# Retention by quarters of the array from the fifth chunk on, and one block's two layers interleaved

## The chip, the cores and the metric

One core of a Trainium2 chip. The metric is the device time of one execution in microseconds (us); the kernel before was run three times. Engines: TensorE (PE) multiplies, its weight loads beside it (PEld), VectorE (DVE), ScalarE (ACT), GpSimd (POOL), SyncE (SP), which here only issues DMA transfers.

## The reference

```python
def _attn_ref(q, k, v):                    # 8 batches, 8 heads, 576 tokens, 64 wide
    scores = scale * np.matmul(q, k.transpose(0, 1, 3, 2))
    gamma = 1.0 - 2.0 ** (-5.0 - np.arange(H))
    Dmat = np.where(rel >= 0, gamma ** rel, 0.0)        # rel = position i - position j
    return np.matmul(scores * Dmat, v)

def _moe_ref(x, w_in, w_out):              # x: 4608 tokens x 512; w_in 512 x 2048; w_out 2048 x 512
    h = x @ w_in
    return (h * np.cos(h)) @ w_out

def reference(**kwargs):
    attn_out = _attn_ref(...)              # retention, per batch and head
    x = attn_out.transpose(0, 2, 1, 3).reshape(4608, 512)
    return _moe_ref(x, moe_w_in, moe_w_out)
```

Retention with decay is computed in chunks of tokens: a token sees its own chunk through masked scores, and everything before through a state (a 64 x 64 matrix per head) that is carried from chunk to chunk and begins anew with each batch. The decay is folded into q (`UQ`) and v (`WV`).

## The kernel before

**Work and tiling.** The 4608 tokens are 36 chunks of 128 (`g` = 0 to 35) and 9 blocks of 512 (`j` = 0 to 8). A batch has 576 tokens, so a batch ends within a chunk or a block. Retention writes its output, transposed, in bf16 into the ring `XT` (1536 tokens). A block's first layer is `mlp1(j, dt)` for 16 strips `dt` of `w_in`: four matmuls into one PSUM bank, then ACT's `Sin(h + pi/2)` into `CB`, then DVE's product with h into `GT`. The second layer is `plain2` in blocks 0 and 1 (16 groups of four matmuls, four open outputs, each of which holds a bank), and `mlp2` from block 2 on, seven half-size products instead of eight with sums prepared by DVE (`ssum`, and `tsum` for the weights). First-layer groups take turns through the banks of `MM` (four) that no output holds; `take` and `free` move them.

**Two forms of retention.** Batches 0 and 1 (`b`, chunks `r` = 0 to 4, the last of 64 tokens) run with whole-chunk matmuls: `scores`, `rest` (outputs), `state_mm` and `state_copy`. Their k and q arrive as "quads" (`quad`: four neighbouring tokens per partition, so a packet holds 1 KB), are cast (`quad_cast`), turned by PE (`quad_turn`), and k is turned back by PE (`back`), since the state needs it both ways. The chunk of 64 tokens is turned by `turn`, or by DMA.

From chunk `G0` = 9 on a chunk is loaded by `load_g` (one row of 256 B per token and head), cast by POOL (`casts_g`: k, q, v), turned by a DMA on SP's queue (`turn_dma`), and computed by `quarters(g, n)`, called through `visit`: the array works as four 64 x 64 parts; in one call the outputs of chunk `g` and the scores and state of chunk `n` = g + 1 are woven together. Afterwards DVE masks two halves of the scores and adds two states, ACT copies two halves of the outputs to `XT` (`xt`) and casts two states to bf16 (`SM`, `SN`); these steps wait in `todo` and are put out by `flush`. The next visit reads the scores and the states.

**What sets the order.** Each engine runs its instructions in the order in which `emit` writes them; semaphores tie the engines. SP's queue holds loads and turns in one order. `pump` puts out pending loads as far as loading buffers (16) are free and no more than `AHEAD` = 9 of them (12 later) hold data not yet cast; three make a chunk. `prep(g)` is casts, turn and pump. In block 0's second layer the order is a table by group number `n` (casts, turns, scores of batch 1); in block 1's first layer strips are split at token 192 or 320 around batch 1's `rest`; in block 1's second layer a visit follows groups 1, 5, 9 and 13. In block `j` >= 2 two visits stand in the first layer, after strips 4 and 10, and two in `mlp2`, ahead of product 6 and ahead of product 4.

```python
            if fn == self.load_g and sum(self.busy) + n > (AHEAD if a[0] < 4 * 4 + 2 else AHEAD + 3):
                return
...
        for dt in range(16):
            self.mlp1(j, dt)
            self.flush(2)
            self.steps1(j, dt)
            if dt % 3 == 0 and dt < 12:
                self.prep(g + 3 + dt // 3)
            if dt in (4, 10) and g < NG:
                self.visit(g + dt // 6)
```

Of the kernel before, what the change touches and what calls it, by code (L numbers as in the profile page):

```python
# [13 lines left out]
DM = H_ * D_  # L14
# [10 lines left out]
AHEAD = 9  # L25
SLOT = (0, 1, 2, 3, 8, 4, 5, 6, 7)
G0 = 9
# [6 lines left out]
def slot(b, r):  # L34
    return SLOT[(NCH * b + r) % NR]

# [4 lines left out]
def gslot(g):  # L41
    return SLOT[(g - G0 + 2 * NCH) % NR]

# [4 lines left out]


def ck_of(r):  # L50
    return min(CH, S_ - CH * r)
# [92 lines left out]
class _Kernel:  # L144
# [154 lines left out]
    def load(self, b, r, xs="kqv"):  # L299
        ck = ck_of(r)  # L300
        for x in xs:
            src = bass.AP(self.src[x], (b * H_ * S_ + CH * r) * D_, [[D_, ck], [S_ * D_, H_], [1, D_]])
            self.fetch((x, b, r), src, [[D_, H_], [1, D_]], ck)
# [18 lines left out]
    def quad(self, x, b, c):  # L322

        src = bass.AP(self.src[x], (b * H_ + 2 * c) * S_ * D_, [[4 * D_, 128], [S_ * D_, 2], [1, 4 * D_]])
        self.fetch((x, b, "c", c), src, [[4 * D_, 2], [1, 4 * D_]], 128)
# [21 lines left out]
    def kcast(self, eng, b, r):  # L347
        ck, i = ck_of(r), slot(b, r)
        t, bt = self.use(("k", b, r))
        o, a = bass.AP(self.KQ[i], 0, [[2 * DM, ck], [1, DM]]), bass.AP(t, 0, [[DM, ck], [1, DM]])  # L350
        self.copy(eng, o, a, [bt], [self.bKB[i]])

    def casts_g(self, g):
        i, r = gslot(g), column(g)
        t, bt = self.use(("k", g))
        h4 = [[DM, CH], [4 * D_, 2], [D_, 4], [1, D_]]
        self.copy("pool", self.heads(self.KQ[i], 0, 2 * DM, CH), bass.AP(t, 0, h4), [bt], [self.bKB[i]])
# [3 lines left out]
        self.s.op("pool", lambda e: e.tensor_tensor(o, a, w, ALU.mult), reads=[bt, self.bUQ], writes=[self.bQB[i]])  # L361
# [3 lines left out]
        self.s.op("pool", lambda e: e.tensor_tensor(o2, a2, w2, ALU.mult), reads=[bt, self.bWV], writes=[self.bVB[i]])  # L365
# [5 lines left out]
    def decay(self, eng, x, b, r):  # L371
        ck, i = ck_of(r), slot(b, r)
        t, bt = self.use((x, b, r))
        d, off, pitch, bd, w, bw = ((self.KQ[i], DM, 2 * DM, self.bQB[i], self.UQ, self.bUQ) if x == "q"
                                    else (self.VB[i], 0, DM, self.bVB[i], self.WV, self.bWV))
        o, a, g = (bass.AP(d, off, [[pitch, ck], [D_, H_], [1, D_]]), bass.AP(t, 0, [[DM, ck], [D_, H_], [1, D_]]),
                   bass.AP(w, r * H_, [[2 * NCH * H_, ck], [1, H_], [0, D_]]))
        self.s.op(eng, lambda e: e.tensor_tensor(o, a, g, ALU.mult), reads=[bt, bw], writes=[bd])  # L378
# [4 lines left out]
    def casts(self, b, r, engs=("pool", "pool", "pool")):  # L383
        self.kcast(engs[0], b, r)
        self.decay(engs[1], "q", b, r)
        self.decay(engs[2], "v", b, r)

    def turn_dma(self, i, ck=CH):
        s = self.s
        s.dma("sp", f"t{i}", lambda e: e.dma_start_transpose(  # L390
            self.kqt(i, 0, ck, 2 * NP), bass.AP(self.KQ[i], 0, [[2 * DM, ck], [1, 2 * DM]])),
            reads=[self.bKB[i], self.bQB[i]], writes=[self.bKT[i], self.bQT[i]])

    def turn(self, b, r, x, eng, bank=None):
        ck, i = ck_of(r), slot(b, r)
        off, c0, bs, bd = (0, 0, self.bKB[i], self.bKT[i]) if x == "k" else (DM, NP, self.bQB[i], self.bQT[i])
        m, bm = bank or self.bank()
        self.group([(bass.AP(m, c * CH, [[512, 128], [1, ck]]),
                     bass.AP(self.KQ[i], off + c * 128, [[2 * DM, ck], [1, 128]]),
                     bass.AP(self.ID, 0, [[128, ck], [1, ck]]),  # L400
                     dict(start=c == 0, stop=c == NP - 1)) for c in range(NP)],
                   [bs, self.bID], [bm])
        self.copy(eng, self.kqt(i, c0, ck, NP), bass.AP(m, 0, [[512, 128], [CH, NP], [1, ck]]), [bm], [bd])

    def quad_cast(self, eng, x, b, c):

        t, bt = self.use((x, b, "c", c))
# [12 lines left out]
    def quad_turn(self, x, b, c, i, eng, bank=None):  # L420
# [6 lines left out]
        s0 = slot(b, 0)  # L427
        off = s0 * W + (c if x == "k" else NP + c) * CH
        t = self.copy(eng, bass.AP(self.KQT, off, [[NR * W, 128], [W, 4], [4, 32], [1, 4]]),
                      bass.AP(m, 0, [[512, 128], [32, 4], [1, 32], [CH, 4]]), [bm], [Buf()])  # L430
        for u in (self.bKT if x == "k" else self.bQT)[s0:s0 + 4]:
            u.w.append(t)

    def back(self, b, r, eng, bank=None):

        i = slot(b, r)
# [33 lines left out]
    def scores(self, b, r, own=True):  # L470
        s, ck, i = self.s, ck_of(r), slot(b, r)
        sc, bsc = zip(*(zip(self.SC, self.bSC) if own else [self.bank(), self.bank()]))
        mms = []
        for c in range(NP):
            for hp in range(2):
                base = 64 * hp * NR * W + i * W + c * CH
                mms.append((
                    bass.AP(sc[hp], c * CH, [[512, ck], [1, ck]]),
                    bass.AP(self.KQT, base, [[NR * W, 64], [1, ck]]),
                    bass.AP(self.KQT, base + NP * CH, [[NR * W, 64], [1, ck]]),  # L480
                    dict(start=c == 0, stop=c == NP - 1)))
        self.group(mms, [self.bKT[i], self.bQT[i]], list(bsc))
        for hp in range(2):
            p3 = [[512, ck], [CH, NP], [1, ck]]
            s.op("dve", lambda e: e.tensor_tensor(
                bass.AP(self.RT[r % 2][hp], 0, p3), bass.AP(sc[hp], 0, p3),
                bass.AP(self.MK, 0, [[CH, ck], [0, NP], [1, ck]]), ALU.mult),
                reads=[bsc[hp], self.bMK], writes=[self.bRT[r % 2][hp]])

    def rest(self, b, r, bank=None, eng="act", state=True):  # L490
# [19 lines left out]
        if r:  # L510
            reads += [self.bSB[(r - 1) % 2], self.bQT[i]]
# [590 lines left out]
```

## Time and profile before

| | us |
|---|---|
| median of three runs | 296.84 (296.74 to 297.48) |
| the profiled execution | 296.34 |
| its span, first to last instruction | 294.6 |
| PE busy | 283.1 |
| DVE busy | 215.0 |
| ACT busy | 173.2 |
| POOL busy | 94.2 |

The profiled execution ran 0.5 us under the median, and 1.74 us of it lie outside the span. Matmuls are pipelined and their ends modelled, so PE's busy time is no measure of its work; the distance between the starts of groups is. In the timelines a row gives start, length, engine, line, operation, output and inputs, shape and count; brackets give the idle time before it and what ended it. In the rows of DMA queues stand packets, MB and the share of the 16 DMA engines' time: q0 carries the weights, q1 SP's loads and turns, q10 the output. In rows of windows the last three columns are the granted clock, DMA share and GB/s.

### The profile page before, as it was taken

To read this page: it belongs to the slowest core of one execution; us is meant where nothing else is said; L and a number is where in the kernel's file an instruction comes from. 1 tells how busy PE (TensorE), PEld (TensorE's weight loads), DVE (VectorE), ACT (ScalarE), POOL (GpSimd) and SP (SyncE) were. 2 spreads that over 40 slices of the span, in tenths; PEclk is the share of its full clock that TensorE was granted. 3 is DMA by queue.
4 is the path that set the end of the run, shared out by engine and by line. 5 is a ranking of instruction groups with operands and counts; after the bars stand their busy time and mean duration, and the time that the engine had idled before them with its cause. 6 is when DMAs were issued, how large, how long until landed. Compare 5 with 4: busy or idle time off the path is not lost.

```text
span 294.6 us, 8326 instructions
## 1 busy us (share of the span) xinstructions
PE 283.1 (96%) x3523; PEld 180.3 (61%) x3554; DVE 215.0 (73%) x466; ACT 173.2 (59%) x344; POOL 94.2 (32%) x119
## 2 busy tenths in 40 slices
PE   6899999899999999999999999999999999999996
PEld 3474455555554478547854785478547854784485
DVE  3667657767766797579758975897589658956973
ACT  6798424887446854585458445844585358536720
POOL 3570227664516520760076007600760030000000
PEclk9999999999999999999999999999999999999999
DMA  6999999999999999999999957997690170013013
GB/s 210 258 181 198 217 312 198 311 187 185 229 201 235 204 198 229 257 202 188 200 242 230 180 136 169 199 189 164 181 181 0 38 145 2 3 36 109 0 38 107
DMA packets 142325, 49.70 MB, mean 169 GB/s; under 512 B 125904, under 2 KB 141264, under 8 KB 142288
## 3 DMA queue, kind: packets, MB, share of 16 engines
q1 hardware_dynamic: 129280, 35.53, 64.4%
q10 hardware_dynamic: 8784, 9.44, 10.1%
q0 software_dynamic: 4224, 4.19, 8.7%
q8 instruction: 28, 0.46, 0.7%
q14 instruction: 9, 0.07, 0.1%
HBM read 36.70 MB, written 9.44 MB: 157 GB/s over the span
## 4 chain that ended last, share of the span: by engine, by line
PE 78%; DMA 13%; SPq 2%; ACT 2%; issue 1%; POOL 1%; DVE 1%; DVEq 0%
PE mm L461 52%; PE mm L463 17%; DMA ld<-in_v_dram 7%; DMA ld<-in_q_dram 4%; PE st L709 3%; PE sc L709 2%; SPq L290 2%; DMA win<-in_moe_w_in_dram 2%; PE po L709 2%; POOL vb L378 1%; PE sc L461 1%; ACT sb L342 1%; PE sc L463 0%; ACT xt L342 0%; ACT kq L342 0%
## 5 line engine op out<-in xcount | busy, mean ns | idle before, releaser
L554 DVE TENSOR_TENSOR gt<-mm,cb 128x512 bf16<-128x512 f32 (+3 forms) x156 | 99.1, 646 | 33.2 <-ACT cb L552 32.4
L552 ACT ACTIVATE cb<-mm,c_pih 128x512 bf16<-128x512 f32 (+3 forms) x156 | 100.6, 654 | 36.4 <-PE mm L463 35.7
L461 PE MATMUL mm<-xt,win 128*128 128x512 bf16 (+3 forms) x445 | 113.3, 362 | 2.8 <-issue 1.9
L461 PEld LDWEIGHTS mm<-xt,win 128*128 128x128 bf16 x468 | 43.4, 98 | 45.2 <-ACT xt L342 0.6
L463 PE MATMUL mm<-xt,win 128*128 128x512 bf16 (+3 forms) x156 | 56.6, 363 | 0.1
L342 POOL CAST kq<-ld 128x512 bf16<-128x512 f32 (+1 forms) x29 | 17.7, 609 | 113.8 <-PE mm L463 96.5
L461 PE MATMUL mm<-wout,gt 128*128 128x256 bf16 (+1 forms) x257 | 49.3, 310 | 1.0 <-issue 1.0
L461 PE MATMUL mm<-ts,ss 128*128 128x256 bf16 x240 | 35.4, 273 | 0.0
L461 PEld LDWEIGHTS mm<-wout,gt 128*128 128x128 bf16 x264 | 24.8, 98 | 12.0 <-DVE gt L554 0.4
L342 ACT ACTIVATE u<-mm 128x512 f32<-128x512 f32 x21 | 12.5, 597 | 32.2 <-PE mm L463 32.2
L361 POOL TENSOR_TENSOR kq<-ld,uq 128x512 bf16<-128x512 f32 x27 | 28.1, 1042 | 6.0 <-DMA ld<-in_q_dram 6.0
L365 POOL TENSOR_TENSOR vb<-ld,wv 128x512 bf16<-128x512 f32 x27 | 28.3, 1049 | 4.1 <-DMA ld<-in_v_dram 4.1
L643 DVE TENSOR_TENSOR osb<-mm,u 128x512 f32<-128x512 f32 x20 | 13.8, 688 | 18.8 <-PE mm L463 11.2
L463 PE MATMUL mm<-wout,gt 128*128 128x256 bf16 (+1 forms) x88 | 27.4, 311 | 0.0
L342 ACT ACTIVATE xt<-po 128x256 bf16<-128x256 f32 (+1 forms) x34 | 14.0, 413 | 21.9 <-PE st L709 15.7
L463 PEld LDWEIGHTS mm<-xt,win 128*128 128x128 bf16 x156 | 15.2, 98 | 16.0
L461 PEld LDWEIGHTS mm<-ts,ss 128*128 128x128 bf16 x240 | 23.0, 98 | 2.8
L750 DVE TENSOR_TENSOR rt<-sc,mh 128x256 bf16<-128x256 f32 x54 | 21.2, 416 | 4.4 <-PE st L709 3.2
L463 PE MATMUL mm<-ts,ss 128*128 128x256 bf16 x80 | 21.8, 273 | 0.0
L576 DVE TENSOR_TENSOR ss<-gt 128x512 bf16<-128x512 bf16 x56 | 20.7, 417 | 0.0
L760 DVE TENSOR_TENSOR pf<-sc,pf 128x256 f32<-128x256 f32 x42 | 17.6, 419 | 1.1
L709 PE MATMUL po<-rt,vb 64*64 64x64 bf16 x216 | 13.4, 202 | 0.1
(155 smaller groups left out, 384.1 us busy)
## 6 DMA issues: line engine op xcount, KB each, us to landing
out_dram<-osb ACTq DMA_DIRECT2D x35, 256.0 KB, 3.3
ld<-in_k_dram SPq DMA_DIRECT2D x32, 256.0 KB, 4.4
ld<-in_q_dram SPq DMA_DIRECT2D x32, 256.0 KB, 5.0
ld<-in_v_dram SPq DMA_DIRECT2D x32, 256.0 KB, 5.9
win<-in_moe_w_in_dram POOLq DMA_DIRECT2D x4, 512.0 KB, 6.1
wout<-in_moe_w_out_dram POOLq DMA_DIRECT2D x4, 512.0 KB, 15.0
ld<-in_k_dram SPq DMA_DIRECT2D x8, 128.0 KB, 4.1
ld<-in_q_dram SPq DMA_DIRECT2D x8, 128.0 KB, 3.9
```

Of the source, the lines that this page charges most:

```text
L342: fn = (lambda e: e.activation(o, x, AF.Copy)) if eng == "act" else (lambda e: e.tensor_copy(o, x))
L361: self.s.op("pool", lambda e: e.tensor_tensor(o, a, w, ALU.mult), reads=[bt, self.bUQ], writes=[self.bQB[i]])
L365: self.s.op("pool", lambda e: e.tensor_tensor(o2, a2, w2, ALU.mult), reads=[bt, self.bWV], writes=[self.bVB[i]])
L461: self.nc.tensor.matmul(o, a, b, **kw)
L463: return s.done("pe", self.nc.tensor.matmul(o, a, b, **kw), reads, writes)
L552: s.op("act", lambda e: e.activation(ci, mi, AF.Sin, bias=self.C_PIH.ap(), scale=1.0), reads=[bm, self.bC], writes=[self.bCB[i]])
L554: s.op("dve", lambda e: e.tensor_tensor(bass.AP(self.GT, dt * TB + o0, [[16 * TB, 128], [1, n]]), mi, ci, ALU.mult), reads=[bm, self.bCB[i ...
L576: self.s.op("dve", lambda e: e.tensor_tensor(self.s_(k, d), a, b, op), reads=rd, writes=[S[k - 1][p]])
L643: self.s.op("dve", lambda e: e.tensor_tensor(o, m, x, ALU.add), reads=[bm, self.bU[u]], writes=[self.bOSB[i]])
L709: inst = self.nc.tensor.matmul(o, a, c, **kw)
L750: s.op("dve", lambda e: e.tensor_tensor(bass.AP(self.RT[n % 2][x], 0, p3), bass.AP(self.SC[x], 0, p3), bass.AP(self.MH, 0, [[64, 128], [0, ...
L760: s.op("dve", lambda e: e.tensor_tensor(self.PF[t].ap(), u, self.PF[1 - t].ap(), ALU.add), reads=[self.bSU[t], self.bPF[1 - t]], writes=[s ...
```

## The change

Batch 0 keeps its first four chunks in the whole-chunk form; its state then passes to the quarters' form (`state_over`, four small ACT copies). From chunk 4 on (`G0` = 4) every chunk is loaded by `load_g` and computed by `quarters`. Chunks 4 and 5 are turned by PE, all later ones by DMA. The quads, turns back, scores and outputs of batch 1 in the whole-chunk form are gone. Blocks 0 and 1 now hold ten visits instead of four: chunk 4's scores, 4 with 5, and 5's outputs in block 0's second layer; then seven in block 1 (V5 to V11, the first only the scores and state of chunk 6).

Block 1's layers are interleaved by an order written out: `F` is the first layer for the first 256 tokens of a strip, `S` for the second 256, `P` a quarter of an output's sum in the second layer, `V` a visit with the `prep` of the chunk three further, `T` a weight sum, `O` the store of an output kept back. Outputs of block 0 go to `U` and `OSB` and are stored later, the last of them during block 2's first layer. Prefetch is 12 buffers, 6 and 12 again, by chunk. In block 2 the visits stand at strips 9 and 15, ahead of product 4 and behind it; in block 3 at strips 7 and 12 and as before. At the start, POOL's decay of chunk 2's v stands behind the second to fourth loads of `w_in` instead of between them.

```diff
-AHEAD = 9
-SLOT = (0, 1, 2, 3, 8, 4, 5, 6, 7)
-G0 = 9
+def ahead(g):
+    return 12 if g < 8 else 6 if g < 21 else 12
+G0 = 4
...
+ORDER1 = """
+F0 F1 F2 F3 F4 F5 F6 P00 F7 F8 F9 F10 V5 P01 F11 F12 F13 F14 F15 P02 T0 P10 T1 P11 V6 P12 T2 P03 T3 P13
+V7 S0 S1 S2 S3 S4 S5 S6 P20 V8 S7 S8 S9 S10 P21 O3 S11 S12 V9 S13 S14 S15 P22 T4 P30 T5 P31 V10
+P32 O0 T6 P23 T7 O0 V11 P33
+"""
...
+    def state_over(self, eng):
+        sn, bsn = self.SN[(G0 - 1) % 2], self.bSN[(G0 - 1) % 2]
+        ws = []
+        for b in range(2):
+            for hp in range(2):
+                ws.append(self.copy(eng, bass.AP(sn, 64 * b * NP * D_ + hp * D_, [[NP * D_, 64], [2 * D_, 2], [1, D_]]),
+                                    bass.AP(self.ST, 64 * hp * 512 + 2 * b * D_, [[512, 64], [D_, 2], [1, D_]]),
+                                    [self.bST], [Buf()]))
+        bsn.w = ws
...
     def mlp2(self, j, visits):
+        def visit(k):
+            if k in visits:
+                self.visit(visits[k])
+                self.flush(6)
...
-        for g in visits[:1]:
-            self.visit(g)
-        self.flush(6)
+        visit(2)
         self.product(bs, 6, False, False)
...
-        for g in visits[1:]:
-            self.visit(g)
-        self.flush(6)
+        visit(7)
         if not last:
             self.product(bs, 4, False, True)
             i21 = self.osb()
...
+        visit(4)
         self.store(i22, j, 1, 1)
...
         for n in range(16):
-            self.plain2(0, n % 4, n // 4, None)
+            self.plain2(0, n % 4, n // 4)
+            if 2 <= n < 10:
+                self.tsum("dve", *T.pop(0))
+            if n == 7:
+                self.turn(4, "k", "act", XY[0])
+                self.turn(4, "q", "dve", XY[1])
+                self.casts_g(5)
+            if n == 11:
+                self.quarters(None, 4)
+                self.flush()
+            if n == 13:
+                self.turn(5, "k", "act", XY[0])
+                self.turn(5, "q", "dve", XY[1])
+                o += [self.out2(0, st, eng) for st, eng in ((0, "act"), (1, "dve"))]
+                for g in (6, 7):
+                    self.casts_g(g)
+                    self.turn_dma(g)
                 self.pump()
+            if n == 14:
+                self.quarters(4, 5)
+                self.flush()
             if n == 15:
+                self.quarters(5, None)
+                self.flush()
+                o += [self.out2(0, st, eng) for st, eng in ((2, "dve"), (3, "act"))]
...
+        for u in ORDER1.split():
+            n = int(u[1:])
+            if u[0] == "V":
+                self.quarters(n if n > 5 else None, n + 1)
+                self.prep(n + 3)
+            elif u[0] == "P":
+                self.plain2(1, n // 10, n % 10)
+                if n % 10 == 3:
+                    o.append(self.out2(1, n // 10, "act"))
+            elif u[0] == "O":
+                self.put2(*o.pop(n))
+            elif u[0] == "T":
+                self.tsum("dve", *T[n])
+            else:
+                m1([n], (0 if u[0] == "F" else 256, 256), 1)
+            self.flush(4)
+        self.flush()
         for j in range(2, NTB):
             g = 4 * j + 4 if j < NTB - 1 else NG
+            at = {2: (9, 15), 3: (7, 12)}.get(j, (4, 10))
             for dt in range(16):
                 self.mlp1(j, dt)
                 self.flush(2)
                 self.steps1(j, dt)
+                if o and dt % 3 == 1:
+                    self.put2(*o.pop(0))
...
-                if dt in (4, 10) and g < NG:
-                    self.visit(g + dt // 6)
-            self.mlp2(j, range(g + 2, min(g + 4, NG)))
+                if dt in at and g < NG:
+                    self.visit(g + at.index(dt))
+            self.mlp2(j, {} if g == NG else dict(zip((7, 4) if j == 2 else (2, 7), (g + 2, g + 3))))
```

More of the change, by code (lines that the diff above doesn't have):

```diff
@@ L468, in idle, with scores @@
                      dict(start=True, stop=True)) for _ in range(n)], [self.bIDLE], [bm])
-    def scores(self, b, r, own=True):
-        s, ck, i = self.s, ck_of(r), slot(b, r)
+    def scores(self, r, own=True):
+        s = self.s
         sc, bsc = zip(*(zip(self.SC, self.bSC) if own else [self.bank(), self.bank()]))
@@ L510, in rest @@
         if r:
[L511 removed]
+            reads += [self.bSB[(r - 1) % 2], self.bQT[r]]
         self.group(mms, reads, [bpo])
[L513 to L522 removed]
@@ L890, in pump @@
             else:
-                n = 3 if fn == self.load_g or fn == self.load and len(a) == 2 else 1
+                n = 3 if fn == self.load_g else 1
                 if any(self.busy[(self.n_ld + i) % NL] for i in range(n)):
                     return
-                if fn == self.load_g and sum(self.busy) + n > (AHEAD if a[0] < 4 * 4 + 2 else AHEAD + 3):
+                if fn == self.load_g and sum(self.busy) + n > ahead(a[0]):
                     return
```

313 lines of the change are left out of this document (103 added, 210 removed).

## The prediction

> **What bounds the kernel now.** I read the page first, then the stage boundaries in the timeline of TensorE (PE), then one stage piece by piece, then the DMA queues by window. The page:
>
> ```profile
> span 294.6 us, 8326 instructions
> PE 283.1 (96%) x3523; PEld 180.3 (61%) x3554; DVE 215.0 (73%) x466; ACT 173.2 (59%) x344; POOL 94.2 (32%) x119
> PEclk9999999999999999999999999999999999999999
> ```
>
> PE is the bound, at full clock. "Busy 96%" does not say that it works at its peak, so I price the change by the starts of matmul groups. Boundaries, from the timeline of PE and, for the last two, the chain of waits:
>
> ```profile
> 33.12 0.81 PE L461 MATMUL mm<-wout,gt 128*128 128x512 bf16 x3
> 33.98 0.81 PE L461 MATMUL mm<-wout,gt 128*128 128x512 bf16 x3
> 54.51 0.41 PE L461 MATMUL mm<-xt,win 128*128 128x192 bf16 x3
> 72.27 0.81 PE L461 MATMUL mm<-wout,gt 128*128 128x512 bf16 x3
> 89.26 0.81 PE L461 MATMUL mm<-xt,win 128*128 128x512 bf16 x3
> 148.21 0.59 PE mm L461 x2
> 177.62 0.59 PE mm L461 x2
> ```
>
> Block 0's second layer starts at 33.12, block 1's first layer at 54.51, its second at 72.27, block 2 at 89.26. One group of four 512-column matmuls takes 0.864 us (33.12 to 33.98). From block 2 on, a block takes 29.41 us (148.21 to 177.62), with four visits; the change leaves that rhythm alone except in block 2. So the time is decided by when block 2 starts, plus what block 2 loses. Before 33.12 the changed program keeps PE's order; POOL's third decay and the weight loads swap places in one queue, and four ACT copies replace two, each beside first-layer groups with free ACT time. I cost that at nothing; if a weight load came late it would be tenths.
>
> The pieces, from the timelines of PE, ACT and DVE:
>
> ```profile
> 20.66 0.49 PE L461 MATMUL mm<-xt,win 128*128 128x256 bf16 x3
> 21.09 0.49 PE L461 MATMUL mm<-xt,win 128*128 128x256 bf16 x3
> 21.31 1.77 ACT L552 ACTIVATE cb<-mm,c_pih 128x256 bf16<-128x256 f32 x4
> 21.82 1.72 DVE L554 TENSOR_TENSOR gt<-mm,cb 128x256 bf16<-128x256 f32 x4 [0.43 <-ACT cb L552]
> 42.14 0.33 PE L461 MATMUL po<-ident,qs 128*128 128x128 bf16 x3
> 42.59 0.81 PE L461 MATMUL mm<-wout,gt 128*128 128x512 bf16 x3
> 82.16 0.38 PE L463 MATMUL mm<-wout,gt 128*128 128x512 bf16 x1
> 82.47 0.22 PE L709 MATMUL st<-rt,vb 64*64 64x64 bf16 x2
> 83.13 0.76 DVE L750 TENSOR_TENSOR rt<-sc,mh 128x256 bf16<-128x256 f32 x2 [0.95 <-PE st L709]
> 83.44 0.59 PE L461 MATMUL mm<-wout,gt 128*128 128x512 bf16 x2 [0.16 <-issue]
> 83.44 0.38 ACT L342 ACTIVATE xt<-po 128x256 bf16<-128x256 f32 x1 [1.93 <-PE st L709]
> 83.72 0.38 ACT L342 ACTIVATE xt<-st 128x256 bf16<-128x256 f32 x1
> 83.81 0.94 DVE L760 TENSOR_TENSOR pf<-sc,pf 128x256 f32<-128x256 f32 x2
> 84.25 0.42 ACT L342 ACTIVATE sm<-pf 128x256 bf16<-128x256 f32 x1 [0.16 <-DVE pf L760]
> L342 ACT ACTIVATE osb<-mm 128x512 f32<-128x512 f32 x12 | 7.1, 595 | 7.2 <-PE mm L463 7.2
> ```
>
> Read from them: a 256-column first-layer group takes 0.437 us of PE. Its bank is free 1.61 us after its start: Sin begins 0.645 later (20.66 to 21.31), the product 0.51 after that, and lasts some 0.43. Two turns by PE (eight 128-column matmuls) take 0.45 (42.14 to 42.59). A whole visit takes 0.85: the group at 82.16 ends its slot at 82.38, and the next group, whose first record is missing, started one matmul before 83.44, at 83.22. From a visit's start (82.47) its tokens stand in XT after 1.64 (83.72 + 0.38) and the state SM after 2.2 (84.25 + 0.42).
>
> **The change, part by part.** *Block 0's second layer.* Before, 33.12 to 54.51 is 21.4 us, of which the 16 groups are 13.8. The rest is batch 1's turns back and forth, four chunks' scores and waits. After: 13.8; turns of chunks 4 and 5 by PE, 2 x 0.45; scores and state of chunk 4 alone, about 0.45 (half a visit); one whole visit 0.85; the outputs of chunk 5 alone, about 0.5. That is 16.5. Two waits are new: the last visit needs the state of the visit one group (0.864) earlier, which takes 2.2, so it stands some 0.5; and block 1's first group needs the tokens of that visit, 0.9 after PE could go on (1.64 against 0.75 of visit). Block 1 starts at 33.12 + 16.5 + 1.4 = 51.0, so **3.5 us earlier**.
>
> *Block 1.* Before, 54.51 to 89.26 is 34.75. After: 32 halves x 0.437 = 14.0; 16 groups x 0.864 = 13.8; the first visit (scores only) 0.5 and six whole ones x 0.85 = 5.1; together 33.4. The stalls follow from the order written out. Four banks at 1.61 sustain one half in 0.40, under PE's 0.437; but each open output holds one, and three banks sustain only one in 0.54. So F10, the fourth half behind P00, stands 0.3. After a visit DVE adds for 0.94 and ACT then casts two states (0.42 each) ahead of the queued Sins, while PE runs ahead: F14 and F15 stand 0.9 together, S5 and S6 0.6 (the visit before them adds and casts one state, not two), S10 0.4, S12 0.4. S0 follows its visit directly and stands 0.9 for the tokens. In all 3.5; block 1 takes 36.9, **2.15 us more**. Block 2 would start at 51.0 + 36.9 = 87.9, against 89.26.
>
> *Block 2.* Its last visit is moved behind product 4. The casts of the visit before are queued on ACT behind the copy of that product's result (0.6, queued until the product ends), and the last visit's past part needs SM: 0.6 + 0.4 after the product's end, where PE gets there after 0.5. **0.6 us**. The delayed stores cost ACT only issue time, beside its slack; the visits at dt 9 and 15 cost what they cost elsewhere.
>
> *DMA.* The last chunk that block 1 needs turned is 12, for the visit V11. Rows of the DMA queues by window (24 to 36, 57 to 79, 80 to 92), POOL's arrivals, and two windows of all engines:
>
> ```profile
> q0 software_dynamic: 1802, 1.78, 87.7%
> q1 hardware_dynamic: 1803, 0.66, 32.8%
> 28.93 0.60 POOL L342 CAST kq<-ld 64x512 bf16<-64x512 f32 x1 [7.53 <-DMA ld<-in_k_dram]
> 31.96 1.03 POOL L378 TENSOR_TENSOR kq<-ld,uq 64x512 bf16<-64x512 f32 x1 [2.42 <-DMA ld<-in_q_dram]
> 35.23 1.06 POOL L378 TENSOR_TENSOR vb<-ld,wv 64x512 bf16<-64x512 f32 x1 [2.23 <-DMA ld<-in_v_dram]
> q1 hardware_dynamic: 17213, 4.31, 93.9%
> q1 hardware_dynamic: 7097, 1.78, 109.5%
> q10 hardware_dynamic: 400, 0.72, 17.2%
> 36.00:44.00 8.00, 7.84 (x72) 4.25 (x72) 3.92 (x8) 1.76 (x5) 2.13 (x4) 1.00 1.15 306
> 60.00:72.00 12.00, 11.59 (x85) 6.49 (x82) 8.35 (x19) 9.78 (x21) 7.00 (x8) 1.00 0.96 196
> ```
>
> While the weights load (q0), the input queue (q1) gets one packet for each of theirs, 150 a microsecond: 512 packets every 3.0 to 3.3 us (28.93, 31.96, 35.23). Chunk 4 is now whole, 1024 packets for each of k, q, v (128 tokens x 8 heads of 256 B): k at 32.0, q at 38.3, cast by 39.4, and its turn by PE stands at 33.12 + 8 x 0.864 = 40.0. In time. v follows between 39.6 (at 782 a microsecond) and 45 (at 150); the 306 GB/s of 36 to 44 says that the weights end in it, and I take 41. Chunks 5 to 7 take 3 x 3072 packets at 782 a microsecond (17213 in 22 us), until 52.8; chunk 5's q lands near 43.6 and is wanted at 46. From there to chunk 12 turned lie six loads (8 to 13, since each turn is issued behind the next load) and seven turns, 18432 + 7168 = 25600 packets: 32.7 us, until 85.5; one output store (0.72 MB took 17.2% of 12 us, so 0.75 for 256 KB) and the landing add 1.1: 86.6. V11 stands at 51.0 + 35.3 = 86.3. So DMA and PE meet: I take 0.3 us of wait. Both ends: nothing, if 800 or more packets pass in a microsecond; at the 591 of 80 to 92 (7097 in 12 us, stores among them) 25600 packets take 43 us, 10 us late. I take the value near 782, since that window is as full of loads and turns and has almost no stores, as block 1 will.
>
> Against the change speaks the size of the packets: batch 1's k and q came as 1 KB packets and now come as 256 B; the window with 1 KB packets moved 306 GB/s beside the weights, the one without 196. The counts above hold that already. The Trainium skill, page "DMA: Bandwidth & Descriptors", section Specifications, puts the smallest transfer at line rate at 512 B, with a read-modify-write below it; the trace agrees in direction, 0.64 of the rate. By that rule alone (half of 306, an estimate) the five chunks' 2.6 MB of k and q would take 17 us where 196 GB/s gives 13.4, so V11 would wait some 4 us and the sum be 3.5 us worse, which is the late turns below at their far end.
>
> Sum: -3.5 + 2.15 + 0.6 + 0.3 = -0.45 us. The profiled execution took 296.34 us, 1.74 beyond its span and 0.5 under the median of the three runs, 296.84. I forecast against the median: **296.4 us**, no change that can be told; a measurement of this kernel can tell about 0.3%, 0.9 us.
>
> **The rivals.** *Turned chunks late (slower).* A turn waits for POOL's casts, sits in one queue with the loads, and now only two chunks are ahead where three were. For it: the sum meets at the edge already, and 80 to 92 was slower. Against it: SP's own issues fit. It decides below 780 packets a microsecond. At 745, 34.4 us bring chunk 12 at 88.3, 2.0 late: 298.1. At 715, the mean of both windows (24310 in 34 us), 3.4 late: 299.5.
>
> *The stalls in block 1 are smaller (faster).* The 2.6 us of bank waits come from queue orders that I followed step by step; if ACT's casts slip between the Sins, they go. Then V11 stands at 83.7, and DMA decides: at 830 packets a microsecond chunk 12 comes at 52.8 + 30.8 + 1.1 = 84.7 and 1.0 of wait comes back, with none of the 0.3: 296.4 - 2.6 - 0.3 + 1.0 = 294.5. Against it: the in-order queues leave little choice.
>
> *The head start doesn't come.* Chunk 4 or 5 late by 1 to 2 us, and block 1 starts at 52.5: 297.9.
>
> **How the numbers follow.** The forecast with its edges (295.6 to 297.3) 0.42; late turns 0.27; smaller stalls 0.26; no head start 0.05. Faster by over 0.3%: 0.25 of the third case and 0.07 of the forecast's lower edge, 0.32. Slower: nearly all late turns and half of the last, 0.28. Within: 0.40. Range 294.4 to 299.5: from just under the faster rival's time to the late turns at 715.
>
> **What would show it.** Right: block 1's first group at 51.0 +- 0.5, block 2's at 87.6 to 88.6, gaps of some 0.9 before F0 and S0, waits of ACT's and DVE's making at F10, F14, S5, and a gap of some 0.6 in block 2's last visit. Wrong by late turns: PE waiting in V7 to V11 for the turn's DMA. Wrong by the stalls: block 2 before 86.5. Wrong at the start: a first-layer group of block 0 not at its old time, or block 1 after 52.

## The result, and the profile after

The changed kernel takes 298.3 us (median of 11 executions, 297.25 to 299.72) against 296.73 us before (11 executions, 296.18 to 299.65): a ratio of 1.0051 [1.0026, 1.0076], slower by half a per cent. Timed once more on another occasion it was 298.73 against 296.44, 1.0068 [1.0040, 1.0096]. The forecast was 296.4, no change that can be told. The profiled execution took 297.25 us, 0.91 more than the profiled one before; it is the fastest of its 11, so 1.05 us of the median is not in it.

The head of the page after, and its input queue:

```profile
span 295.5 us, 8651 instructions
PE 284.7 (96%) x3694; PEld 180.6 (61%) x3694; DVE 215.9 (73%) x473; ACT 171.9 (58%) x351; POOL 97.4 (33%) x120
PEclk9999999999999999999999999999999999999999
q1 hardware_dynamic: 138048, 36.19, 68.9%
```

Nothing here tells where 0.9 us went: PE is the bound as before, at full clock. The boundaries and stalls do, from the timeline of PE (start, duration, work; in brackets what it waited for last):

```profile
50.89 0.50 PE L445 MATMUL mm<-xt,win 128*128 128x256 bf16 x3 [0.76 <-ACT xt L343]
...
56.45 0.28 PE L445 MATMUL mm<-xt,win 128*128 128x256 bf16 x1 [0.15 <-DVE gt L541]
...
60.84 0.28 PE L445 MATMUL mm<-xt,win 128*128 128x256 bf16 x1 [0.36 <-DVE gt L541]
...
69.04 0.39 PE L445 MATMUL mm<-xt,win 128*128 128x256 bf16 x2 [0.84 <-ACT xt L343]
...
72.28 0.28 PE L445 MATMUL mm<-xt,win 128*128 128x256 bf16 x1 [0.33 <-DVE gt L541]
...
87.87 0.39 PE L445 MATMUL mm<-xt,win 128*128 128x512 bf16 x1
...
112.04 0.50 PE L445 MATMUL mm<-ts,ss 128*128 128x256 bf16 x3 [0.57 <-DVE ss L563]
...
118.82 0.38 PE L445 MATMUL mm<-xt,win 128*128 128x512 bf16 x1
...
132.11 0.22 PE L692 MATMUL po<-kqt,sn 64*64 64x64 bf16 x2 [0.24 <-ACT sm L343]
...
148.87 0.38 PE L445 MATMUL mm<-xt,win 128*128 128x512 bf16 x1
```

Block 1 starts at 50.89 (54.51 before), and block 2 at 87.87 (89.26 before), 1.4 us earlier. Then block 2 takes 30.95 us and block 3 30.05, where they took 29.62 and 29.33 (and the later blocks 29.41 to 29.50); at 148.87 the kernel is 0.66 behind the one before (148.21), and from there every block takes what it took. So the gain was made where it was forecast, and given back, with interest, in the next two blocks. The row at 112.04 is a wait that the prediction doesn't have: 0.74 us by the distance between starts, where the bracket has 0.57, because it counts from the modelled end of the matmul before (waits without a row below are by starts, too). What was going on beside it, in the timeline of all engines:

```profile
109.21 3.11 DVE L563 TENSOR_TENSOR ss<-gt 128x512 bf16<-128x512 bf16 x4
...
109.42 1.10 POOL L356 TENSOR_TENSOR kq<-ld,uq 128x512 bf16<-128x512 f32 x1 [0.43 <-DMA ld<-in_q_dram]
...
110.48 1.22 POOL L360 TENSOR_TENSOR vb<-ld,wv 128x512 bf16<-128x512 f32 x1
```

Four of DVE's sums for product 7 take 3.11 us, where four without POOL beside them take 1.42 (a row of it below), while POOL multiplies q and v of chunk 17, which have just come from the DMA. The groups of DVE's sums from 100 to 146 us, first after, then before (busy time, mean ns of one):

```profile
L563 DVE TENSOR_TENSOR ss<-gt 128x512 bf16<-128x512 bf16 x16 | 8.1, 559 | 0.0
```

```profile
L576 DVE TENSOR_TENSOR ss<-gt 128x512 bf16<-128x512 bf16 x16 | 5.8, 418 | 0.0
```

And the windows of the second layers of blocks 2 and 3 (the column with 6.95 and 3.47 is POOL's busy time), first after, then before:

```profile
104.00:118.80 14.80, 13.88 (x236) 11.52 (x235) 13.24 (x31) 5.47 (x14) 6.95 (x7) 1.00 1.21 212
...
133.00:148.80 15.80, 15.80 (x242) 12.84 (x241) 12.78 (x33) 7.56 (x17) 3.47 (x4) 1.00 1.17 217
```

```profile
104.70:118.90 14.20, 14.15 (x242) 12.32 (x242) 11.48 (x31) 5.66 (x14) 0.86 (x1) 1.00 1.23 214
...
134.00:148.20 14.20, 14.16 (x234) 12.24 (x234) 11.60 (x31) 5.79 (x14) 0.00 (x0) 1.00 1.25 211
```

Before, the DMA was far enough ahead that POOL had nearly all its casts done in a block's first layer, where DVE forms only two of a block's sixteen sums, behind strip 14. The changed kernel's loads run later against its blocks, and POOL casts when the data come: in the second layer, beside the sums. None of the 112 sums in the profile before has a POOL operation beside it; in the profile after nine have.

The theories from here: **A**, the loss is work that the new order and the later loads put beside each other in blocks 2 and 3 (ACT's casts ahead of close visits, POOL's casts beside sums); **B**, in executions slower than the profiled one, turned chunks come late and PE waits for them in block 1.

### The profile page after: what moved, and what is told of

Read it like the earlier page. It is cut to its first block, busy times and chain, and to the rows that moved or that the text cites. A ratio compares the mean times of both kernels' runs of the same rounds, so it can differ in the third digit from the quotient of the medians.

```text
span 295.5 us, 8651 instructions
## 1 busy us (share of the span) xinstructions
PE 284.7 (96%) x3694; PEld 180.6 (61%) x3694; DVE 215.9 (73%) x473; ACT 171.9 (58%) x351; POOL 97.4 (33%) x120
## 4 chain that ended last, share of the span: by engine, by line
PE 86%; DVE 7%; ACT 3%; issue 1%; DMA 1%; POOL 0%; DVEq 0%; ACTq 0%; POOLq 0%
PE mm L445 58%; PE mm L447 19%; PE st L692 3%; PE sc L692 3%; DVE gt L541 2%; DVE ss L563 2%; PE po L692 2%; ACT cb L539 1%; DMA ld<-in_k_dram 1%; PE sc L445 1%; DVE rt L471 1%; DVE rt L733 1%; DVE pf L743 1%; ACT xt L343 1%; PE sc L447 0%
## 5 line engine op out<-in xcount | busy, mean ns | idle before, releaser
L541 DVE TENSOR_TENSOR gt<-mm,cb 128x512 bf16<-128x512 f32 (+1 forms) x164 | 100.7, 622 | 37.9 <-ACT cb L539 36.9
L539 ACT ACTIVATE cb<-mm,c_pih 128x512 bf16<-128x512 f32 (+1 forms) x164 | 102.3, 634 | 37.9 <-PE mm L447 37.1
L445 PE MATMUL mm<-xt,win 128*128 128x512 bf16 (+1 forms) x492 | 119.2, 354 | 3.0 <-ACT xt L343 1.6
L445 PEld LDWEIGHTS mm<-xt,win 128*128 128x128 bf16 x492 | 45.8, 98 | 47.6 <-DVE gt L541 3.5
L447 PE MATMUL mm<-xt,win 128*128 128x512 bf16 (+1 forms) x164 | 57.9, 353 | 0.0
L343 POOL CAST kq<-ld 128x512 bf16<-128x512 f32 x32 | 19.7, 615 | 110.8 <-PE mm L447 72.6
L356 POOL TENSOR_TENSOR kq<-ld,uq 128x512 bf16<-128x512 f32 x32 | 33.5, 1047 | 16.5 <-DMA ld<-in_q_dram 16.5
L360 POOL TENSOR_TENSOR vb<-ld,wv 128x512 bf16<-128x512 f32 x32 | 34.2, 1068 | 8.1 <-DMA ld<-in_v_dram 7.7
L733 DVE TENSOR_TENSOR rt<-sc,mh 128x256 bf16<-128x256 f32 x64 | 24.8, 415 | 4.5 <-PE st L692 2.2
L447 PEld LDWEIGHTS mm<-xt,win 128*128 128x128 bf16 x164 | 16.0, 98 | 15.1
L743 DVE TENSOR_TENSOR pf<-sc,pf 128x256 f32<-128x256 f32 x49 | 20.5, 418 | 1.1
L692 PE MATMUL po<-rt,vb 64*64 64x64 bf16 x256 | 15.9, 202 | 0.2
```

The lines of the kernel that those rows point to most:

```text
L343: fn = (lambda e: e.activation(o, x, AF.Copy)) if eng == "act" else (lambda e: e.tensor_copy(o, x))
L356: self.s.op(engs[1], lambda e: e.tensor_tensor(o, a, w, ALU.mult), reads=[bt, self.bUQ], writes=[self.bQB[i]])
L360: self.s.op(engs[2], lambda e: e.tensor_tensor(o2, a2, w2, ALU.mult), reads=[bt, self.bWV], writes=[self.bVB[i]])
L445: self.nc.tensor.matmul(o, a, b, **kw)
L447: return s.done("pe", self.nc.tensor.matmul(o, a, b, **kw), reads, writes)
L539: s.op("act", lambda e: e.activation(ci, mi, AF.Sin, bias=self.C_PIH.ap(), scale=1.0), reads=[bm, self.bC], writes=[self.bCB[i]])
```

## The experiments

"Changed" is the changed kernel; medians are in us, ratios against the kernel before, with intervals.

**The changed kernel again** (no edit), once for another profile and once timed.

> The changed kernel once more, for another profile. Its executions lay between 297.25 and 299.7 and the profile at hand is the fastest. Theory B: in an execution at 298.3 or above the added time is PE waiting for turned chunks in V9 to V11 or in block 2's first visits, 1 us or more. Theory A: the same gaps as before in blocks 2 and 3, a little longer.

> The changed kernel unchanged, timed beside the next two, as their base: 298.3 within 0.4, executions between 297 and 300.

The first took 298.75 us, the second a median of 298.73 (297.4 to 303.63, two of its eight over 300). In the first one's profile block 1 is the same to 0.2 us and V11 doesn't stand; the difference is block 3, which took 31.56 us instead of 30.05:

```profile
135.77 1.04 POOL L356 TENSOR_TENSOR kq<-ld,uq 128x512 bf16<-128x512 f32 x1 [2.18 <-DMA ld<-in_q_dram]
...
136.02 2.25 DVE L563 TENSOR_TENSOR ss<-gt 128x512 bf16<-128x512 bf16 x2
...
136.77 1.22 POOL L360 TENSOR_TENSOR vb<-ld,wv 128x512 bf16<-128x512 f32 x1
...
138.20 0.68 DVE L541 TENSOR_TENSOR gt<-mm,cb 128x512 bf16<-128x512 f32 x1
...
138.93 0.50 PE L445 MATMUL mm<-wout,gt 128*128 128x256 bf16 x3 [0.75 <-DVE gt L541]
```

Two sums take 2.25 us beside POOL, the last first-layer product is queued behind them on DVE, and PE stands for that product. So A held in this execution: what the first profile lacks is the same collision once more, in block 3.

**V7 one group earlier**, by itself, once more for a profile, and with an earlier load.

```diff
-... P03 T3 P13 V7 S0 S1 ...
+... P03 T3 V7 P13 S0 S1 ...
```

> In the order of block 1 the visit V7 stands one group earlier, ahead of P13 instead of behind it, so S0 no longer follows its visit directly. If the wait of S0 for the visit's tokens is a real loss: 1.0 us of gap at 69.0 goes, block 2 starts 0.9 us earlier (86.9), the median falls to 297.4. If the DMA sets V11 (chunk 12 turned at 85.3, then V11 wanted at 85.3): the gain turns up as a wait at V11 and block 2 starts where it did, 298.3.

> The kernel with V7 ahead of P13 once more, for another profile: its executions lay at 296.7 once and at 301 to 305 five times, and the profile at hand is of the first kind. If this profile is of the second kind: theory B has PE wait 4 to 7 us in block 1's visits for turned chunks, most of it at V11 or just before; its rival has the time spread over gaps behind ACT and DVE.

> Both single edits together: V7 ahead of P13, and load 8 between the turns of chunks 6 and 7. Alone, the first took a median of 302.05 us (one execution in six at 296.7), the second 297.5. Theory B (turned chunks come late in most executions, the visit order only sets how little room there is): the earlier load gives back 1 us of room, and the median falls well below 302, to 297 to 299. Rival (V7's new place costs PE, ACT or DVE time by itself): the earlier load changes nothing of that, the median stays at 301 to 302.

Alone, a median of 302.05, 1.0208 [1.0165, 1.0251], from only six executions, one of 296.74 and five of 301.07 to 304.8; they are too far apart for a firm ratio. But an edit that takes a 1.0 us wait out of PE's order made five of six executions over 2 us slower than the changed kernel's 298.73. Its two profiles are of executions of 296.74 and 303.37 us. PE's row at V11 in the first, in the second, and two windows of the second (the third column from the right is the granted clock):

```profile
85.23 0.26 PE L692 MATMUL sc<-kqt 64*64 64x64 bf16 x8 [0.66 <-DMA kqt<-kq]
```

```profile
90.30 0.33 PE L692 MATMUL sc<-kqt 64*64 64x64 bf16 x8 [4.51 <-DMA kqt<-kq]
```

```profile
80.00:90.00 10.00, 5.58 (x95) 2.87 (x94) 5.01 (x14) 3.82 (x10) 3.36 (x4) 0.98 1.02 174
90.00:95.00 5.00, 4.37 (x69) 2.45 (x71) 1.51 (x4) 2.47 (x7) 1.92 (x3) 0.70 1.12 218
```

V11's scores wait for the turned chunk 12, 0.66 us in the one execution and 4.51 in the other. After the long wait the granted clock of PE was 0.70 for 5 us. The 80 to 90 window moved 174 GB/s. So theory B is seen as well: chunk 12 landed at 85.19 in one execution and 90.25 in another of the same kernel. With the earlier load added the median was 297.31 (295.85 to 301.66), 1.0015 [0.9994, 1.0036], with one execution of twelve over 300: the new place of V7 costs nothing by itself that shows, the loads decide. (The same edit in the versions below brings its gain as far as block 2.)

**The earlier load by itself, and two stores moved away from V11.**

```diff
                     self.turn_dma(g)
-                self.pump()
+                    self.pump()        # load 8 between the turns of chunks 6 and 7
```

```diff
-P32 O0 T6 P23 T7 O0 V11 P33
+P32 T6 P23 T7 V11 P33
...
-                if o and dt % 3 == 1:
+                if o and dt % 2 == 1:
```

> Load 8 is issued between the turns of chunks 6 and 7 instead of behind both, which fills the 1 us hole of the DMA queue at 51.2. Theory A: no stall of the changed kernel hangs on the DMA, the time stays at 298.3 within 0.3. Theory B: all turned chunks of block 1 come some 1 us earlier, the spread of the executions shrinks and the median falls by 0.6 to 1 us, to 297.3 to 297.7.

> Two of the three output stores of 256 KB that block 1 issues (just before V11) move to block 2, where the seven left are issued at every second strip. Theory B (the input queue is at its limit and V11 waits for chunk 12): 1.5 us of transfers leave the stretch before V11, so the wait at V11 shrinks; median 297.3 to 297.9 against the changed kernel's 298.3, with a narrower spread. Rival (the lateness lies earlier, in the loads of chunks 8 to 10, or has nothing to do with the DMA): 298.3, spread as before.

The load: 297.52 (296.62 to 298.49), 1.0028 [1.0013, 1.0043], 0.8 under the changed kernel and with a narrower spread, as B has it, though the intervals overlap. The stores: 298.06, 1.0048 [1.0028, 1.0068], within what the changed kernel does; in that profile chunk 12 landed at 85.31 with the stores away, 85.28 with them. That the two stores make chunk 12 late is not borne out.

**ACT's order of casts.** Block 3's visits back to dt 4 and 10; and in block 2 the casts ahead of product 4's copy.

```diff
-            at = {2: (9, 15), 3: (7, 12)}.get(j, (4, 10))
+            at = (9, 15) if j == 2 else (4, 10)
```

```diff
             self.product(bs, 4, False, True)
+            if j == 2:
+                self.flush()
```

> Block 3's two visits go back to dt 4 and 10 (the changed kernel has 7 and 12). Theory A (the loss is visits that stand too close for ACT's state casts): the gap of 0.7 us in block 3's second visit goes, block 3 takes 29.4 us instead of 30.05, the median is 0.6 us under the changed kernel's 298.3, so 297.7. Theory B (turned chunks come late from the DMA queue in most executions): chunk 17 is now wanted at 122.3 instead of 125 and chunk 18 at 127.5 instead of 131, so the visits wait for turns instead; no gain, and the executions keep their spread of 2.5 us.

> In block 2, ACT's casts of the states of the visit behind product 7 are queued ahead of the copy of product 4's result instead of behind it. If the gap of 0.6 us in block 2's last visit is that queue order (as predicted): both gaps there (116.1 and 116.8, together 0.67) go, and the median falls by 0.6 to 297.7. If the visit stands for DVE's late additions instead: one gap of 0.3 to 0.4 stays, 298.0.

The first: block 3 takes 29.41 us in its profile (119.34 to 148.75), exactly the old rhythm, so the 0.64 of the first profile was the visits at 7 and 12, only five strips apart. (Block 3 takes 30.05 or 30.06 in three more profiles that have these visits and no sum that holds PE up there.) The median was 297.37, 1.0036 [1.0011, 1.0061]; that lies 0.9 under the changed kernel's, but the intervals overlap. The second: of the two gaps in block 2's last visit (0.28 and 0.39, worked out from starts) the 0.39 went and the 0.28 stayed. In the changed kernel they stood so:

```profile
115.85 0.60 ACT L343 ACTIVATE osb<-mm 128x512 f32<-128x512 f32 x1 [1.21 <-PE mm L447]
...
116.35 0.41 ACT L343 ACTIVATE sm<-pf 128x256 bf16<-128x256 f32 x1
...
116.81 0.22 PE L692 MATMUL po<-kqt,sn 64*64 64x64 bf16 x2 [0.23 <-ACT sm L343]
```

The cast sits behind the copy, and the past part (the outputs' share that comes from the state) behind the cast; the other gap is DVE's additions ahead of the scores. Its median, 298.01, 1.0039 [1.0016, 1.0063], doesn't tell 0.4 us from none. Its profile shows the late turn in an order of block 1 that is the changed kernel's own:

```profile
88.06 0.32 PE L692 MATMUL sc<-kqt 64*64 64x64 bf16 x16 [2.29 <-DMA kqt<-kq]
```

**POOL's casts and DVE's sums, moved apart, brought together, made small.** In the changed kernel the casts of chunks 17 and 18 behind the sums for product 7; in the kernel before two chunks' casts put beside the sums, in blocks 4 to 6; in the changed kernel POOL's operations for chunks 16 to 22 on 8 of 64 elements.

```diff
                 self.ssum(3, p)
+        if j == 2:
+            self.s.need("pool", self.bSS[2][3].w)
+            self.prep(17)
+            self.prep(18)
...
-                if dt % 3 == 0 and dt < 12:
+                if dt % 3 == 0 and dt < (6 if j == 2 else 12):
```

```diff
             self.ssum(2, p)
+        if j in (4, 5, 6):                # the kernel before
+            self.s.need("pool", self.bSS[1][3].w)
+            self.prep(4 * j + 9)
+            self.prep(4 * j + 10)
...
-                if dt % 3 == 0 and dt < 12:
+                if dt % 3 == 0 and dt < (6 if j in (4, 5, 6) else 12):
```

```diff
+        d = 8 if 16 <= g <= 22 else D_     # and d for D_ in the tiles of the three operations
```

> In block 2 POOL's casts of chunks 17 and 18 wait until DVE's four sums for product 7 are done. Theory A1 (those sums took 0.78 us each instead of 0.4 because POOL read and wrote SBUF beside them): the sums take 0.4, the gap of 0.74 ahead of product 7 at 112.0 goes, 297.6. Theory A2 (they are slow for another reason, or start late): the sums and the gap stay, 298.3. Turned chunks 17 and 18 come some 2 us later and are wanted 6 us after that, so nothing else should wait.

> The kernel before, with one thing added: in blocks 4, 5 and 6 POOL's casts of the two chunks that are used last are held back to the second layer, beside DVE's sums, where the changed kernel's blocks 2 and 3 have theirs. Theory A1 (a sum with a POOL operation beside it takes 0.75 to 1.0 us instead of 0.42 and DVE's delay reaches PE): the sums of these blocks that have a cast beside them take 0.7 or more, each of the three blocks takes 0.7 to 1.5 us more than 29.4, the time rises by 2 to 4.5 us to 299 to 301. Rival (DVE's slack covers it, the gaps of the changed kernel have another cause): 296.6, within 0.3.

> The changed kernel, but POOL's three operations for each of chunks 16 to 22 work on 8 of the 64 elements of each head (the rest of the tiles keeps old values); all waits and the order stay, and those turns are issued some 2 us earlier. If POOL beside DVE's sums costs what the profiles show in blocks 2 and 3: no sum takes over 0.5 us there, no gap ahead of products 7 or 6, block 2 takes 30.1 and block 3 30.05 in every execution; the median falls by 1.0 to 1.5 us, to 296.8 to 297.3; the late turns at V11 stay. Rival (the sums are late for another reason): 298.3.

Moved: the gap ahead of product 7 went and the four sums took 1.42 us, but the next three, for product 3, took 2.35 beside the casts that now met them; block 2 took 30.6, block 3 31.2 (its casts were later too, and a visit waited some 0.4 us for its turn), and the median was 298.76, 1.0060 [1.0034, 1.0085]. The cost moved with the casts:

```profile
109.59 1.42 DVE L563 TENSOR_TENSOR ss<-gt 128x512 bf16<-128x512 bf16 x4
...
110.93 2.35 DVE L563 TENSOR_TENSOR ss<-gt,ss 128x512 bf16<-128x512 bf16 x3
...
111.08 0.74 POOL L343 CAST kq<-ld 128x512 bf16<-128x512 f32 x1 [5.41 <-DVE ss L563]
```

Brought together, in the kernel before: 299.88, 1.0123 [1.0088, 1.0157], 3.1 us slower with the same instructions on PE, DVE and POOL. The three blocks took 30.71, 30.65 and 30.18 instead of 29.4 to 29.5 (starts of blocks 4 to 7, then the group of those blocks' sums):

```profile
147.98 0.38 PE L461 MATMUL mm<-xt,win 128*128 128x512 bf16 x1
...
178.69 0.38 PE L461 MATMUL mm<-xt,win 128*128 128x512 bf16 x1
...
209.34 0.38 PE L461 MATMUL mm<-xt,win 128*128 128x512 bf16 x1
...
239.52 0.38 PE L461 MATMUL mm<-xt,win 128*128 128x512 bf16 x1
```

```profile
L576 DVE TENSOR_TENSOR ss<-gt 128x512 bf16<-128x512 bf16 x24 | 16.0, 716 | 0.0
```

The same edit also issues turns and loads later. That isn't behind the loss: all waits of PE in these three blocks (total, times, longest) are for sums or of the kind that the profile before has too, and none is for a turned chunk.

```profile
PE mm L461 <- DVE ss L576: 2.3, 5, 0.6
PE mm L461 <- issue: 1.0, 6, 0.2
```

Made small: 296.98, 1.0019 [0.9992, 1.0046], 1.75 under the changed kernel timed beside it, and the sums of 100 to 146 us are back:

```profile
L564 DVE TENSOR_TENSOR ss<-gt 128x512 bf16<-128x512 bf16 x16 | 6.1, 431 | 0.0
```

That profile has no gap ahead of products 6 and 7, and V11 still stands 0.79 us for its turn, as expected; block 2 takes 30.32 and block 3 30.38 (30.1 and 30.05 expected). Some of the 1.75 is that these turns are issued earlier; the two were not tried apart.

**Fewer bytes**, alone and with the small casts.

```diff
+                m = 32 if x == "v" and 8 <= g <= 20 else n    # m for n in load_g's src and dst
```

> The changed kernel, but of v's chunks 8 to 20 only 32 tokens of each piece are loaded (the rest of the tile keeps old values), so that each of these chunks brings 768 packets of 256 B less (512 less where it comes in two pieces). Everything else is issued as before. If the DMA is behind both of the losses that the runs showed (late turns at V11, and casts that arrive beside DVE's sums in blocks 2 and 3): chunk 12 is turned by 82 in every execution, block 2 starts at 87.9 and takes 30.0, block 3 starts its casts early; the median falls by 1.5 to 2 us to 296.3 to 296.8, and the executions lie within 1 us of each other. If the losses belong to the new order of the work itself: 298, with the spread as it was.

> Both cuts together: 32 tokens of each piece of v's chunks 8 to 20 loaded, POOL's operations for chunks 16 to 22 on 8 of 64 elements. Alone, the first gave 297.27 against 298.3. If late turns and casts beside sums are two separate losses and the only ones beyond ACT's queue order: their gains add up, 295.8 to 296.3, and the executions lie within 1 us. If they are one loss: 297.0, as with the first alone.

Alone: 297.27 (296.36 to 298.21), 1.0014 [0.9997, 1.0032], 1.0 under the first timing of the changed kernel, less than expected; chunk 12 was turned 2.7 us before V11 wanted it, but two sums of block 2 still met casts (2.40 us for two) and PE stood 0.98 us there. Both: 296.44 (295.67 to 297.16), 0.9995 [0.9983, 1.0007], 2.3 under the changed kernel and just over what two separate losses would give, with all executions within 1.5 us. Its block 2 starts at 87.90 and takes 30.54 (29.62 before), its block 3 30.06 (29.33 before); the waits of over 0.1 us left there are those of block 2's last visit and of block 3's second.

```profile
118.44 0.38 PE L447 MATMUL mm<-xt,win 128*128 128x512 bf16 x1
...
148.50 0.38 PE L447 MATMUL mm<-xt,win 128*128 128x512 bf16 x1
```

**Versions to beat both.** v1 has V7 earlier, the earlier load, the stores moved, block 3 at 4 and 10, and the casts ahead of the copy. v2 adds this, v3 also the casts behind the sums, with block 3's visits at 5 and 11 and a `flush` behind its first layer:

```diff
-    return 12 if g < 8 else 6 if g < 21 else 12
+    return 12 if g < 8 else 6 if g < 24 else 12
```

> All edits together: V7 ahead of P13, load 8 between the turns, two stores moved to block 2, block 3's visits at dt 4 and 10, the casts ahead of product 4's copy. By theory A and B together: block 2 starts at 87.0 without a wait at V11 in most executions, block 2 takes 30.2 (the sums beside POOL stay), block 3 29.4 to 29.9; against the kernel before that is -2.3 + 0.8 + 0.2 = -1.3 us: a median of 295.3 to 295.8, below the kernel before's 296.6. If the late casts cost more once the visits stand closer, or the DMA is late again: 296.5 to 297.5, no better than before.

> The combined version with one edit more: the far look-ahead of the loads starts at chunk 24 instead of 21, so that the turns of chunks 19 and 20 are not queued behind the nine transfers that bring chunks 20 to 22. In the combined version's profile PE waited 0.97 us for chunk 19 and 0.75 us for chunk 20 in block 3's second layer. If that queue order is the cause: both waits go, block 3 takes 29.4 to 29.9 instead of 31.0, the median falls to 295.0 to 295.6, below the kernel before. If the DMA has no more room to give there (its transfers are the limit up to block 4): the waits stay or come back in block 4, 296.3 to 296.8.

> The second version with the casts of chunks 17 and 18 held back behind DVE's four sums for product 7, and block 3's first two visits at dt 5 and 11, so that the later chunks still come in time. If POOL beside the sums is what is left of block 2's loss: block 2 takes 29.8 instead of 31.2 and the median is 0.6 to 1.2 us under the second version's, 294.0 to 294.9. If the held-back casts only meet other sums or come too late for block 3 (as when this was done alone): the same as the second version or up to 0.5 us more.

v1: 296.63, 0.9997 [0.9981, 1.0012]; v2: 296.78, 0.9997 [0.9975, 1.0019]; v3: 297.36, 1.0016 [0.9992, 1.0039]. All come out under the changed kernel, and none can be told from the one before. v1's block 2 starts at 86.03, 3.2 us earlier than before, and its block 4 at 148.20, the very time of before (148.21): on the way it loses 1.2 us to sums beside casts in block 2, and in block 3 PE waits for turned chunks 19 and 20:

```profile
137.13 0.32 PE L692 MATMUL sc<-kqt 64*64 64x64 bf16 x16 [0.81 <-DMA kqt<-kq]
```

```profile
143.85 0.29 PE L692 MATMUL sc<-kqt 64*64 64x64 bf16 x12 [0.59 <-DMA kqt<-kq]
```

v2 takes these two waits away, and in their place sums meet casts in block 3 (gaps of 0.74 and 0.25). v3 takes the collision away from product 7 of block 2; the sums behind it meet the casts instead (PE stands 0.92 us at that block's last visit), and so do those of block 3. Each of these edits lets PE arrive earlier at data that come when the DMA brings them.

## Why the prediction was wrong, by its own steps

**Right.** Block 0's second layer: block 1's first group forecast at 51.0, measured at 50.89; the two terms it hung on are there, its wait for tokens (0.9 forecast, 0.92 between the slots) included. Block 1: 36.9 forecast, 36.98 measured, and the stalls stand where they were put: F10 0.3 (measured 0.32), F14 and F15 0.9 (0.85), S0 0.9 (1.01), S5 and S6 0.6 (0.49), S10 0.4 (0.44), S12 0.4 (0.32). Block 2's start: 87.9 to 88.2 forecast, 87.87 measured. Its last visit: 0.6 forecast, 0.67 measured, though only 0.39 of that is the queue order named; the rest is DVE's additions, so that this number was right in part by luck.

**Wrong, first: "The change leaves that rhythm alone except in block 2".** The sentence wasn't checked against the diff's own line, which moves block 3's visits to dt 7 and 12. Their five strips are too few for DVE's additions and ACT's casts to leave their queues, much what was priced for block 2; it costs 0.64 us, and block 3 at 4 and 10 shows it as 0.

**Wrong, second: block 2 is "0.6 us" and "the visits at dt 9 and 15 cost what they cost elsewhere".** The step priced the visits and left out POOL. The DMA paragraph asked of every late load only whether PE would wait for the turned chunk. It didn't ask where POOL's casts of the late chunk would fall, and POOL was taken as an engine with time to spare. The casts fell beside DVE's sums: 0.74 of the 0.95 us that block 2 took beyond the forecast in the first profile (the other 0.2 is that block 2 took 29.62 before, not the 29.41 of later blocks); in other executions the same in block 3, up to 1.5. This is the larger part of the miss, as far as the runs can part it: making the casts small gives back 1.75 of the 2.3 us between the changed kernel and the one before, some of it perhaps through the earlier turns; and in the kernel before, such casts alone cost 3.1.

**Wrong in size, third: the DMA term, "0.3 us of wait" at V11.** None of the three profiles of the changed kernel has this wait. In the first one chunk 12, forecast at 86.6, landed at 85.28, and V11 began its scores at 86.10; what it stood there, some 0.2, was for DVE's additions (85.38 + 0.87):

```profile
85.38 0.87 DVE L743 TENSOR_TENSOR pf<-sc,pf 128x256 f32<-128x256 f32 x2
...
86.10 0.51 PE L692 MATMUL sc<-kqt 64*64 64x64 bf16 x16
```

But with the changed kernel's own block 1 in a kernel edited elsewhere the wait was 2.29 in one profile and 0.79 in another, so a single number was wrong. The rate taken, 782 packets a microsecond, is one execution's; chunk 12 landed anywhere from 85.3 to 88.0 there, and at 90.25 with V7 earlier. The rival that priced this, the late turns at 298.1 to 299.5, gave the right time partly by luck, with half of the mechanism: late data, but what they cost came through casts beside DVE's sums more often than through V11. With casts small and bytes fewer, the kernel takes 0.9995 [0.9983, 1.0007] of before; the forecast's sum, -0.45 us without the DMA's 0.3 and with block 3's 0.64, is -0.1. So the sum of PE's order agrees with that kernel within the noise; what it met was not in it.

The Trainium skill, page "SBUF — State Buffer", section "Who interferes with whom", says that a VectorE instruction with two SBUF inputs contends with a GpSimd instruction that reads SBUF, and that one with at most one, outside of the 2-port modes, does not; the port pair that the two share is an exclusive lock. The traces agree: the sums (two SBUF inputs) go from 0.42 us to a mean of 0.74 for the seven that have over 0.2 us of a POOL operation beside them in the changed kernel, 1.26 at the most, while DVE's product of the first layer (one input from PSUM) takes 0.685 us alone and 0.688 with POOL beside it (each from all such operations after 90 us). Had this been laid beside POOL's arrival times, the second step would have had its rival, though not its price.

## What to carry to other kernels

When a change shifts a stage against its loads, ask of each late transfer not only who waits for it, but what runs when it lands and which engine that work stands beside; an engine with two thirds of its time free can still hold up another one. When several edits each take a wait out and the end doesn't move, look for what arrives at its own time: v1 gained 3.2 us by block 2 and had none of it at block 4. And a wait that an edit removes just ahead of late data is no gain: with V7 earlier V11 waited 0.66 us in one execution and 4.51 in another, with a lower clock behind it. V7's place asks for chunk 12 about 1 us earlier; why it came 5 us later in the second execution stays open.

## What the runs showed of the hardware

- Sums of two bf16 tiles in SBUF on DVE beside POOL's multiplications of f32 tiles: 0.42 us alone, 0.74 to 1.03 as the mean (by profile) of those with over 0.2 us of a POOL operation beside them, 1.28 at the most; POOL's multiplication of v goes from 1.04 (at 90.89 in the profile after) to 1.22 (at 110.48). DVE's product with one input from PSUM stays at 0.685 to 0.688.
- PE's granted clock was 0.70 over the 5 us after a wait of 4.5 us, and 1.00 in the next 5. The Trainium skill, page "TensorE: Matmul & The Clock Gate", Part 1, has the clock at half until some 3.4 us of work have passed; that would be 0.66 over 5 us (an estimate from the page), so the trace agrees.
- The same turned chunk landed 5 us apart in two executions of one kernel (85.19 and 90.25, with V7 earlier), and 2.7 us apart in executions of kernels that issue the same transfers up to there. What makes the transfers of one execution slower wasn't found.
